# Two instead of four weight matrices converted inside attention, and a gated network whose first group runs by chunk over two tiles

## Chip, core and metric

One core of a Trainium2 chip. The metric is the device time of one execution in microseconds; the lower, the better. Three runs of the kernel before gave a median of 986.8 us.

## What is computed

Three stages follow each other on 2304 tokens of width 512 (4 batches of 512 local and 32 global tokens, 8 heads of 64):

```python
out_l = sm(where(|i-j| <= 32, scale * q_l k_l^T, -1e9) ++ scale * q_l k_g^T) @ (v_g ++ v_l)
out_g = sm(scale * q_g (k_g ++ k_l)^T) @ (v_g ++ v_l)
x = out_g ++ out_l                                     # [2304, 512]
x = (sigmoid(x @ w_gate) * (x @ w_val)) @ w_out        # d_ff = 1536
h = x @ w_in                                           # d_ff = 2048
out = (P(h) / (Q(h) + 1e-6)) @ w2_out                  # cubic over quadratic
```

The weights of both networks arrive as 64-bit floats, seen by the kernel as pairs of 32-bit words. Each 128x512 block of them (called a matrix below) is converted on the chip to a high and a low float32r part before it is used.

## The kernel before

Attention runs over 16 units (a batch and a pair of heads). Its steps stand in one table with a place for each (`STEPS`), and the order of issue is unit number plus place, sorted; every engine then works through its instructions in the order of issue. The steps of a matrix's conversion are in the same table and are run for the first `others` units, one matrix per unit: `w_raw` (the load), `w_mag` (two activations, lines 463 and 464), `w_bits` (three VectorE instructions, lines 471 to 473), `w_add` (GpSimd, line 478), `w_hi` (a cast on ScalarE, line 487) and `w_lo` (a subtraction on GpSimd, line 492). `others` is 4 (`Weights.EARLY`).

The gated network runs over 6 groups of two chunks (`G1` = 2 chunks of 128 hidden columns) and within a group over 5 tiles of tokens (two of 512, three of 384). `first(f, i)` makes gate and value of chunk `f` on tile `i`: 12 matmuls each (lines 527 to 529, the third of every three reads the low part of the weights), a sigmoid (554), the product (555), the cast `gh` (558) and the difference `gl` (559). `second(f0, i, gs)` multiplies both chunks of the group by `w_out` (lines 570 to 572) and adds to `gacc` (580 or 582). For tile `i` of a group the order is: `first` of chunk 0, `second` of the tile before, `first` of chunk 1.

Conversions of the matrices that are left run between these. `step()` issues magnitude, bits and add of the next matrix and the load of the one two further on. `finish()` issues `hi` and `lo` of all that are stepped but not yet finished. So the cast of a matrix is issued after the ScalarE instructions of the `first` that was issued before `finish()`. The converted order begins with gate 0, value 0, gate 1, value 1, out 0, out 1; the raw words, `v` and `q` have two buffers each, so the magnitude of a matrix can be written only when `lo` of the matrix two before has read its `v`.

In the trace a name such as `w11gate` is the matrix gate of network 1, chunk 1; `w11out` is that of `w_out`; `pg` and `pv` are the sums of gate and value, `p` those of `second`. `ptl` and `pth` are the low and high parts of the transposed probabilities in attention, `pspv` the sums of probabilities times values, `pss` and `psgl` the scores.

Of the kernel before, what the change touches and what calls it, by code (L numbers as in the profile page):

```python
# [32 lines left out]
TILES = [(0, 512), (512, 512), (1024, 384), (1408, 384), (1792, 384)]  # L33
# [104 lines left out]


KEPT = dict(k=4, q=3, v=2)  # L140


def attention(ctx, tc, ident, xh, xl, ins, other={}, others=0):
# [33 lines left out]
    def load(u, names="kqv"):  # L177

        b, pr = units[u]
        for x in names:  # L180
            if f"{x}n" in st[u]:
                continue
            shape = [128, NBLK, WIN] if x == "k" else [128, NBLK, 128]
            t = st[u][f"{x}n"] = two.tile(shape, F32, tag=f"{x}n", name=f"{x}n{u}", bufs=KEPT[x])
            nc.sync.dma_start(t, ins[f"{x}_l"][b, pr])
# [337 lines left out]
def layer(nc, ps, wh, wl, mh, ml):  # L523

    for k in range(4):
        w = slice(k * 128, (k + 1) * 128)
        nc.tensor.matmul(ps, wh[:, w], mh[:, k], start=k == 0, stop=False)  # L527
        nc.tensor.matmul(ps, wh[:, w], ml[:, k], start=False, stop=False)  # L528
        nc.tensor.matmul(ps, wl[:, w], mh[:, k], start=False, stop=k == 3)  # L529
# [11 lines left out]
def gated(nc, pools, xpool, wp, xh, xl):  # L541
    G = G1
    NF = FF // 128
    acc = [pools.acc.tile([128, 4, n], F32, tag=f"acc{i}", name=f"gacc{i}") for i, (_, n) in enumerate(TILES)]
    yh, yl = [None] * len(TILES), [None] * len(TILES)

    def first(f, i):
        n = TILES[i][1]
        pg = pools.ps1.tile([128, 512], F32, tag="p1", name=f"pg{f}_{i}")
        pv = pools.ps1.tile([128, 512], F32, tag="p1", name=f"pv{f}_{i}")  # L550
        layer(nc, pg[:, 0:n], *wp.have[1, f, "gate"], xh[i], xl[i])
        layer(nc, pv[:, 0:n], *wp.have[1, f, "val"], xh[i], xl[i])
        t = pools.t.tile([128, 512], F32, tag="u", name=f"t{f}_{i}")
        nc.scalar.activation(t[:, 0:n], pg[:, 0:n], AF.Sigmoid)
        nc.vector.tensor_tensor(t[:, 0:n], pv[:, 0:n], t[:, 0:n], ALU.mult)  # L555
        gh = pools.g.tile([128, 512], F32R, tag="gh", name=f"gh{f}_{i}")
        gl = pools.g.tile([128, 512], F32R, tag="gl", name=f"gl{f}_{i}")
        nc.scalar.copy(gh[:, 0:n], t[:, 0:n])  # L558
        nc.vector.tensor_tensor(gl[:, 0:n], t[:, 0:n], gh[:, 0:n].bitcast(F32), ALU.subtract)  # L559
        return gh, gl  # L560

    def second(f0, i, gs):
        n = TILES[i][1]
        ps = [pools.ps2.tile([128, 512], F32, tag="p2", name=f"p2{f0}_{i}_{m}") for m in range(4)]
        for k, (gh, gl) in enumerate(gs):
            wh, wl = wp.have[1, f0 + k, "out"]
            for m in range(4):
                w = slice(m * 128, (m + 1) * 128)
                a, z = k == 0, k == len(gs) - 1
                nc.tensor.matmul(ps[m][:, 0:n], wh[:, w], gh[:, 0:n], start=a, stop=False)  # L570
                nc.tensor.matmul(ps[m][:, 0:n], wh[:, w], gl[:, 0:n], start=False, stop=False)  # L571
                nc.tensor.matmul(ps[m][:, 0:n], wl[:, w], gh[:, 0:n], start=False, stop=z)  # L572
        final = f0 + G == NF
        if final:
            yh[i] = xpool.tile([128, 4, n], F32R, tag=f"xh{i}", name=f"yh{i}")
            yl[i] = xpool.tile([128, 4, n], F32R, tag=f"xl{i}", name=f"yl{i}")
        for m in range(4):
            a = acc[i][:, m]
            if f0 == 0:
                nc.vector.tensor_copy(a, ps[m][:, 0:n])  # L580
            else:
                nc.vector.tensor_tensor(a, ps[m][:, 0:n], a, ALU.add)  # L582
            if final:
                nc.scalar.copy(yh[i][:, m], a)
                nc.gpsimd.tensor_tensor(yl[i][:, m], a, yh[i][:, m].bitcast(F32), ALU.subtract)

    pending = None
    early, jobs = (NF // G - 1) * len(TILES) + 1, len(wp.order) - wp.done
    for f0 in range(0, NF, G):
        for i in range(len(TILES)):  # L590
            k = f0 // G * len(TILES) + i
            more = (k + 1) * jobs // early - k * jobs // early
            gs = [first(f0, i)]
            wp.finish()
            wp.step()
            if pending:
                second(*pending)
            wp.finish()
            for _ in range(more - 2):
                wp.step()  # L600
            gs += [first(f0 + k, i) for k in range(1, G)]
            pending = (f0, i, gs)
            wp.finish()
            wp.step()
            if f0 + G == NF and i > 0:
                for _ in range(2 if i % 2 else 1):
                    wp.load()

    def rest():
        second(*pending)  # L610
        wp.finish()

    return yh, yl, rest
# [154 lines left out]
@with_exitstack  # L768
def tile_kernel(ctx: ExitStack, tc, ins, out):
    nc = tc.nc  # L770
    ctx.enter_context(tc.manual_schedule())
    const = ctx.enter_context(tc.tile_pool(name="const", bufs=1))
    xpool = ctx.enter_context(tc.tile_pool(name="xpool", bufs=1))
    early = ctx.enter_context(tc.tile_pool(name="early", bufs=1))
    ident = const.tile([128, 128], F32, name="ident")
    xh = [xpool.tile([128, 4, n], F32R, tag=f"xh{i}", name=f"xh{i}") for i, (_, n) in enumerate(TILES)]
    xl = [xpool.tile([128, 4, n], F32R, tag=f"xl{i}", name=f"xl{i}") for i, (_, n) in enumerate(TILES)]
    dram = ctx.enter_context(tc.tile_pool(name="dram", bufs=1, space=bass.MemoryType.DRAM))
    wp = Weights(tc, early, dram, {"gate": ins["w_gate"], "val": ins["w_val"], "in": ins["w2_in"]},
                 {1: ins["w_out"], 2: ins["w2_out"]})  # L780

    co = const.tile([128, 8], F32, name="co")
    with ExitStack() as c:
        other = dict(w_raw=wp.fetch, w_mag=wp.magnitude, w_bits=wp.bits, w_add=wp.add, w_hi=wp.hi, w_lo=wp.lo)
        attention(c, tc, ident, xh, xl, ins, other, wp.EARLY)
    wp.done = wp.split = wp.EARLY
    for j in range(2):
        wp.fetch(wp.EARLY + j)

    nc.sync.dma_start(co[:, 0:4], ins["a"].unsqueeze(0).to_broadcast([128, 4]))  # L790
    nc.sync.dma_start(co[:, 4:6], ins["b"].unsqueeze(0).to_broadcast([128, 2]))
    with ExitStack() as c:
        wp.late = c.enter_context(tc.tile_pool(name="late", bufs=1))
        pools = Pools(c, tc)
        wp.staging = pools.t
        yh, yl, rest = gated(nc, pools, xpool, wp, xh, xl)
        rational(nc, pools, wp, yh, yl, rest, co, out)

# [60 lines left out]
```

## Time and profile before

| | |
|---|---|
| median of 3 runs | 986.8 us (986.78 to 986.83) |
| the profiled execution | 987.2 us, span of its instructions 985.3 us |
| TensorE busy | 956.4 us, 97% of the span |
| VectorE, ScalarE, GpSimd busy | 725.4, 622.4 and 556.3 us |
| attention (first score matmul to first gate matmul) | 4.78 to 177.24 us |
| gated network | 177.24 to about 614 us |
| rational network | to 985.3 us |
| mean granted TensorE clock | 0.994 of full speed |

A row of the timeline gives the start, the duration, the engine, the line, the operation, what it writes and reads, and in brackets how long the engine sat idle before it and what ended that. A matmul's duration reaches beyond the start of the next one, since matmuls are pipelined; the distance of two starts is its price.

### The profile page before, as it was taken

To read this page: it belongs to the slowest core of one execution; us is meant where nothing else is said; L and a number is where in the kernel's file an instruction comes from. 1 tells how busy PE (TensorE), PEld (TensorE's weight loads), DVE (VectorE), ACT (ScalarE), POOL (GpSimd) and SP (SyncE) were. 2 spreads that over 40 slices of the span, in tenths; PEclk is the share of its full clock that TensorE was granted. 3 is DMA by queue.
4 is the path that set the end of the run, shared out by engine and by line. 5 is a ranking of instruction groups with operands and counts; after the bars stand their busy time and mean duration, and the time that the engine had idled before them with its cause. 6 is when DMAs were issued, how large, how long until landed. Compare 5 with 4: busy or idle time off the path is not lost.

```text
span 985.3 us, 14544 instructions
## 1 busy us (share of the span) xinstructions
PE 956.4 (97%) x5024; PEld 847.7 (86%) x5024; DVE 725.4 (74%) x1324; ACT 622.4 (63%) x1272; POOL 556.3 (56%) x520
## 2 busy tenths in 40 slices
PE   5999998999999999999999999999999999999996
PEld 4778887789899899899899898888888888888895
DVE  6988887467667676677667435978788888878985
ACT  5898997434444444444444337877777777877783
POOL 4888888534445444454444336644565666656663
PEclk9999999999999999999999999999999999999998
DMA  7546453234444533444344412001300130010111
GB/s 242 165 124 177 135 162 68 81 104 154 130 143 136 169 128 118 139 150 135 126 151 146 171 44 86 1 1 44 129 1 1 65 107 1 22 65 1 65 54 65
DMA packets 56926, 98.62 MB, mean 100 GB/s; under 512 B 5396, under 2 KB 31124, under 8 KB 56852
## 3 DMA queue, kind: packets, MB, share of 16 engines
q1 hardware_dynamic: 56852, 97.69, 31.1%
q8 instruction: 40, 0.66, 0.3%
q14 instruction: 34, 0.28, 0.1%
HBM read 69.62 MB, written 21.23 MB: 92 GB/s over the span
## 4 chain that ended last, share of the span: by engine, by line
PE 77%; DVE 1%; POOL 1%; issue 1%; ACT 1%; POOLq 0%; DVEq 0%
PE rp L721 6%; PE rp L720 6%; PE rp L719 6%; PE rp L529 6%; PE rp L527 6%; PE rp L528 6%; PE pg L527 5%; PE pg L528 5%; PE pg L529 5%; PE pv L528 5%; PE pv L527 5%; PE pv L529 5%; PE p L572 4%; PE p L571 4%; PE p L570 4%
## 5 line engine op out<-in xcount | busy, mean ns | idle before, releaser
L651 POOL TENSOR_TENSOR v<-v,u 128x384 f32<-128x384 f32 (+1 forms) x80 | 96.3, 1204 | 112.3 <-ACT v L647 111.7
L694 POOL TENSOR_TENSOR rgl<-t,rgh 128x384 fp32r<-128x384 f32 (+1 forms) x80 | 96.4, 1205 | 37.4 <-POOL v L651 30.6
L558 ACT CAST gh<-t 128x384 fp32r<-128x384 f32 (+1 forms) x60 | 33.4, 557 | 124.4 <-DVE t L555 124.4
L555 DVE TENSOR_TENSOR t<-pv,t 128x384 f32<-128x384 f32 (+1 forms) x60 | 36.6, 609 | 77.6 <-PE pv L529 73.7
L659 DVE TENSOR_TENSOR t<-rp,t 128x384 f32<-128x384 f32 (+1 forms) x80 | 48.6, 607 | 54.2 <-ACT t L655 53.5
L644 ACT ACTIVATE u<-rp 128x384 f32<-128x384 f32 (+1 forms) x80 | 42.6, 532 | 65.6 <-PE rp L529 65.4
L680 DVE SCALAR_TENSOR_TENSOR v<-v,u 128x384 f32<-128x384 f32 (+1 forms) x80 | 78.9, 987 | 0.0
L684 DVE SCALAR_TENSOR_TENSOR t<-t,co,v 128x384 f32<-128x384 f32 (+1 forms) x80 | 74.0, 925 | 2.8
L559 DVE TENSOR_TENSOR gl<-t,gh 128x384 fp32r<-128x384 f32 (+1 forms) x60 | 39.5, 658 | 37.4 <-ACT gh L558 37.4
L258 ACT ACTIVATE p<-p,mx 128x224 f32<-128x224 f32 x128 | 60.6, 477 | 6.1 <-DVE mx L251 5.7
L647 ACT ACTIVATE v<-u,co 128x384 f32<-128x384 f32 (+1 forms) x80 | 60.3, 754 | 2.7
L668 ACT ACTIVATE u<-v,co 128x384 f32<-128x384 f32 (+1 forms) x80 | 52.7, 659 | 10.1 <-POOL v L651 10.0
L582 DVE TENSOR_TENSOR gacc<-p,gacc 128x384 f32<-128x384 f32 (+1 forms) x100 | 54.8, 602 | 4.6 <-PE p L572 4.6
L655 ACT ACTIVATE t<-rp,co 128x384 f32<-128x384 f32 (+1 forms) x80 | 55.8, 697 | 0.0
L334 DVE TENSOR_TENSOR ptl<-pspt,pth 112x640 fp32r<-112x640 f32 x64 | 51.0, 815 | 6.0 <-ACT pth L330 5.5
L676 DVE SCALAR_TENSOR_TENSOR v<-v,u 128x384 f32<-128x384 f32 (+1 forms) x80 | 55.3, 691 | 0.0
L325 PE MATMUL pspt<-ident,p 128*112 128x128 f32 x256 | 46.3, 281 | 6.8 <-ACT p L258 4.1
L663 DVE SCALAR_TENSOR_TENSOR t<-t,co,rp 128x384 f32<-128x384 f32 (+1 forms) x80 | 52.7, 659 | 0.0
L330 ACT CAST pth<-pspt 112x640 fp32r<-112x640 f32 x64 | 43.4, 686 | 13.6 <-PE pspt L326 13.1
L672 ACT ACTIVATE u<-u,co 128x384 f32<-128x384 f32 (+1 forms) x80 | 51.9, 649 | 0.0
L690 ACT CAST rgh<-t 128x384 fp32r<-128x384 f32 (+1 forms) x80 | 43.5, 544 | 5.6 <-DVE t L684 5.6
L251 DVE CUSTOM_DVE_ANT_0 p<-pss,masks 128x224 f32<-128x224 f32 x128 | 41.1, 382 | 6.2 <-PE pss L242 5.8
(578 smaller groups left out, 3376.1 us busy)
## 6 DMA issues: line engine op xcount, KB each, us to landing
raw2in<-in_w_in SPq DMA_DIRECT2D x16, 512.0 KB, 3.7
raw2out<-in_w_out SPq DMA_DIRECT2D x16, 512.0 KB, 3.6
kn<-in_k_l SPq DMA_DIRECT2D x16, 448.0 KB, 3.7
raw1gate<-in_w_gate SPq DMA_DIRECT2D x12, 512.0 KB, 5.5
raw1val<-in_w_val SPq DMA_DIRECT2D x12, 512.0 KB, 3.6
raw1out<-in_w_out SPq DMA_DIRECT2D x12, 512.0 KB, 3.9
out<-racc SPq DMA_DIRECT2D x17, 256.0 KB, 2.0
qn<-in_q_l SPq DMA_DIRECT2D x16, 256.0 KB, 3.7
```

Of the source, the lines that this page charges most:

```text
L258: nc.scalar.activation(p, p, AF.Exp, bias=s["mx", half][:, n : n + 1], scale=-1.0, accum_out=s["sm", half][:, n : n + 1])
L527: nc.tensor.matmul(ps, wh[:, w], mh[:, k], start=k == 0, stop=False)
L528: nc.tensor.matmul(ps, wh[:, w], ml[:, k], start=False, stop=False)
L529: nc.tensor.matmul(ps, wl[:, w], mh[:, k], start=False, stop=k == 3)
L647: nc.scalar.activation(new(u, "v"), st[u]["u"], AF.Identity, bias=b0, scale=b1)
L651: nc.gpsimd.tensor_tensor(s["v"], s["v"], s["u"], ALU.mult)
L680: nc.vector.scalar_tensor_tensor(s["v"], s["v"], 2.0, s["u"], ALU.subtract, ALU.mult)
L684: nc.vector.scalar_tensor_tensor(s["t1"], s["t1"], a0, s["v"], ALU.add, ALU.mult)
L694: nc.gpsimd.tensor_tensor(s["gl"], s["t1"], s["gh"].bitcast(F32), ALU.subtract)
L719: nc.tensor.matmul(ps, gh[:, w], wh, start=k == 0, stop=False)
L720: nc.tensor.matmul(ps, gh[:, w], wl, start=False, stop=False)
L721: nc.tensor.matmul(ps, gl[:, w], wh, start=False, stop=k == G - 1)
```

## The change

Attention converts gate 0 and value 0 alone (`CONVERTED` = 2); `Weights.EARLY`, which also says how many places of the ring lie in the early pool, stays at 4. Right behind attention, ahead of the gated network's first matmul, two `step()` issue magnitude, bits and add of gate 1 and value 1. The gated network then opens with chunk 0 on tiles 0 and 1 and chunk 1 on tiles 0 and 1, in place of both chunks tile by tile: `first(0, 0)`; `hi` and `lo` of gate 1 and value 1; `step()` of out 0 and out 1; `first(0, 1)`; `hi` and `lo` of out 0 and out 1; `step()` of the next two (gate 2 and the first of the rational network); `first(1, 0)`; `hi` and `lo` of those; one `step()`; `second` of tile 0; `first(1, 1)`. From tile 2 on the loop is as before, with the conversions that are left spread so that they run two ahead and end three tiles sooner.

```diff
+CONVERTED = 2
...
-    pending = None
-    early, jobs = (NF // G - 1) * len(TILES) + 1, len(wp.order) - wp.done
+    gs = [[], []]
+    for g in range(G):
+        for i in range(2):
+            gs[i].append(first(g, i))
+            wp.finish()
+            if g == 0:
+                wp.step()
+                wp.step()
+            if (g, i) == (G - 1, 0):
+                wp.step()
+                second(0, 0, gs[0])
+    pending = (0, 1, gs[1])
+    early, jobs = (NF // G - 1) * len(TILES) - 2, len(wp.order) - wp.done
     for f0 in range(0, NF, G):
         for i in range(len(TILES)):
-            k = f0 // G * len(TILES) + i
-            more = (k + 1) * jobs // early - k * jobs // early
+            k = f0 // G * len(TILES) + i - 2
+            if k < 0:
+                continue
+            more = min((k + 1) * jobs // early + 2, jobs) - min(k * jobs // early + 2 * (k > 0), jobs)
             gs = [first(f0, i)]
             wp.finish()
             wp.step()
-            if pending:
-                second(*pending)
+            second(*pending)
...
-        attention(c, tc, ident, xh, xl, ins, other, wp.EARLY)
-    wp.done = wp.split = wp.EARLY
+        attention(c, tc, ident, xh, xl, ins, other, CONVERTED)
+    wp.done = wp.split = CONVERTED
     for j in range(2):
-        wp.fetch(wp.EARLY + j)
+        wp.fetch(CONVERTED + j)
...
         wp.staging = pools.t
+        for _ in range(2):
+            wp.step()
```

## Rows read from the trace of the kernel before

**Rows 1.** Busy time by engine in two stretches: steady attention, gated network.

```profile
core 0: us, PE busy (x) PEld busy (x) DVE busy (x) ACT busy (x) POOL busy (x), PEclk, DMA share, GB/s
70.00:160.00 90.00, 87.83 (x629) 75.45 (x629) 77.25 (x248) 81.21 (x244) 75.54 (x105) 1.00 0.50 139
177.24:614.00 436.76, 436.36 (x2222) 398.77 (x2222) 273.46 (x447) 194.75 (x351) 196.72 (x158) 1.00 0.39 128
```

**Rows 2.** What TensorE waited for: total, times, longest, all in us.

```profile
PE pspv L343 <- DVE ptl L334: 2.6, 3, 1.8
...
PE pg L527 <- ACT xs L360: 1.2, 1, 1.2
```

**Rows 3.** Timeline of TensorE: the global scores, once in two units.

```profile
26.71 2.25 PE L280 MATMUL psgl<-kn,qgn 128*128 128x512 f32 x8
...
49.48 2.24 PE L280 MATMUL psgl<-kn,qgn 128*128 128x512 f32 x8
...
70.10 2.24 PE L280 MATMUL psgl<-kn,qgn 128*128 128x512 f32 x8
...
147.64 2.24 PE L280 MATMUL psgl<-kn,qgn 128*128 128x512 f32 x8
```

**Rows 4.** Timeline of TensorE around its waits in units 2 to 5.

```profile
37.98 0.45 PE L343 MATMUL pspv<-pth,vb 112*128 112x320 f32 x2
40.26 0.41 PE L343 MATMUL pspv<-ptl,v 112*128 112x320 f32 x1 [1.83 <-DVE ptl L334]
...
41.69 3.36 PE L242 MATMUL pss<-kn,qn 64*128 64x224 f32 x16
...
52.23 0.56 PE L343 MATMUL pspv<-pth,v 112*128 112x320 f32 x2 [0.50 <-DVE ptl L334]
...
63.01 1.78 PE L242 MATMUL pss<-kn,qn 64*128 64x224 f32 x16
```

**Rows 5.** Timeline of VectorE: the bits of gate 1, then a low part.

```profile
36.55 0.40 DVE L471 TENSOR_SCALAR v1gate<-v1gate 128x512 f32<-128x512 f32 x1
36.98 1.04 DVE L472 TENSOR_SCALAR v1gate<-v1gate 128x512 uint32<-128x512 uint32 x1
38.05 1.41 DVE L473 SCALAR_TENSOR_TENSOR v1gate<-raw1gate,v1gate 128x512 uint32<-128x512 uint32 x1
39.39 0.81 DVE L334 TENSOR_TENSOR ptl<-pspt,pth 112x640 fp32r<-112x640 f32 x1
```

**Rows 6.** TensorE busy and its granted clock (third value) in stretches of 2 us.

```profile
38.00:40.00 2.00, 0.43 (x3) 1.00 0.53 123
...
42.00:44.00 2.00, 2.00 (x12) 0.50 0.56 213
...
179.00:181.00 2.00, 2.00 (x10) 1.00 0.00 0
```

**Rows 7.** Timeline of TensorE: `second` of tile 0, both chunks.

```profile
193.73 0.39 PE L570 MATMUL p<-gh,w10out 128*128 128x512 f32 x1
...
196.68 0.39 PE L571 MATMUL p<-gl,w11out 128*128 128x512 f32 x1
197.28 0.50 PE L572 MATMUL p<-gh,w11out 128*128 128x512 f32 x1 [0.22 <-POOL w11out L492]
```

**Rows 8.** Timelines of VectorE, ScalarE and GpSimd: first product, then out 0's conversion.

```profile
183.11 0.69 DVE L555 TENSOR_TENSOR t<-pv,t 128x512 f32<-128x512 f32 x1 [6.70 <-PE pv L529]
...
185.09 0.42 DVE L471 TENSOR_SCALAR v1out<-v1out 128x512 f32<-128x512 f32 x1
...
183.83 0.62 ACT L558 CAST gh<-t 128x512 fp32r<-128x512 f32 x1 [1.50 <-DVE t L555]
184.36 0.67 ACT L463 ACTIVATE v1out<-raw1out 128x512 f32<-128x512 f32 x1
...
188.17 0.62 ACT L487 CAST w10out<-v1out 128x512 fp32r<-128x512 f32 x1 [2.57 <-POOL v1out L478]
...
186.85 1.29 POOL L478 TENSOR_TENSOR v1out<-v1out,q1out 128x512 uint32<-128x512 uint32 x1 [6.21 <-DVE v1out L473]
188.87 1.29 POOL L492 TENSOR_TENSOR w10out<-v1out,w10out 128x512 fp32r<-128x512 f32 x1 [0.73 <-ACT w10out L487]
```

More of the change, by code (lines that the diff above doesn't have):

```diff
@@ L600, in gated @@
                 wp.step()
-            gs += [first(f0 + k, i) for k in range(1, G)]
+            gs += [first(f0 + g, i) for g in range(1, G)]
             pending = (f0, i, gs)
```

## The prediction

> **What bounds the kernel now.** I read the profile in this order: TensorE's waits, the granted clock and busy time by stretch, then the timelines around the two places that the edit touches. The windows by stage show that TensorE sets the pace: it is busy 87.83 of 90 us in steady attention and 436.36 of 436.76 us in the gated network, while VectorE, ScalarE and GpSimd stay at 75 to 81 us of the 90 [rows 1]. So work that is taken off those three engines is worth only what TensorE waits for it, and work that is put on them costs only what TensorE comes to wait. The list of TensorE's waits names the ones in attention that can belong to a conversion: 2.6 us on the low parts `ptl` from VectorE, 1.8 us of it in one piece [rows 2].
>
> **What attention gives back.** The global scores come once in two units, so the distance of their starts is the price of two units. From 70.10 to 147.64 us there are four such distances: 77.54 / 4 = 19.39 us each. The distance from 26.71 to 49.48 is 22.77, that from 49.48 to 70.10 is 20.62 [rows 3]. These two hold the conversions of gate 1 and value 1, and they are 3.38 and 1.23 us above the steady price, together 4.6 us. The timeline says what fills the first. TensorE waits 1.83 us for a `ptl` until 40.26, and soon after the 16 score matmuls at 41.69 take 3.36 us, against 1.78 us at 63.01: another 1.58 us [rows 4]. VectorE is why: the bits of gate 1 stand from 36.55 to 39.39, 2.84 us, right ahead of that `ptl` in its queue [rows 5]. The slow scores are the clock: half speed is granted from 42 to 44 us, right after a stretch of 2 us in which TensorE was busy for 0.43 [rows 6]. In the second distance a wait of 0.50 us for VectorE at 52.23 is visible [rows 4]; the rest of its 1.23 us I can't put down to one row. Removing both conversions takes away two magnitudes, two times three bits, two adds, two casts and two subtractions, and two loads from SP's queue. I give the loads no price: among the conversions' waits on TensorE's list it is `ptl` alone that stands for more than a microsecond [rows 2]; if a load had held units 2 to 5, its share is within the 4.6 us already.
>
> Bounds: at most the whole 4.6 us; at least 3.0, if the clock still falls once in there for some other wait (4.6 less 1.58). The `hi` and `lo` of gate 0 and value 0 still lie in the first distance, so I take 3.4 us of the first and 0.7, somewhat over half, of the second: **4.1 us**.
>
> **What the opening costs.** Before, TensorE ran the opening almost without a wait: `second` of tile 0 lost 197.28 - 196.68 = 0.60 less one pitch of 0.23 (2.95 us for 13 matmuls from 193.73), **0.4 us**, for `lo` of out 1 [rows 7]. That wait goes, since out 1 is now a pass of 5.4 us earlier. TensorE's number of matmuls is unchanged, and so are its starts up to `second` of tile 0 at 193.73, unless something is late. So I follow the conversions in the order of issue, with hand-overs from one view [rows 8]: product to cast 0.72 (183.11 to 183.83), cast to ScalarE's next 0.53, magnitude to bits 0.73 (184.36 to 185.09), bits to add 1.76 (185.09 to 186.85), cast to subtraction 0.70 (188.17 to 188.87), add and subtraction 1.29 each.
>
> The two `step()` ahead of the network cost nothing: ScalarE's next instruction there is the first sigmoid, VectorE sits idle 6.70 us until 183.11, and the bits, from about 178, fit even at 2.84 us each within half a microsecond [rows 5, 8]. GpSimd's two adds end near 184.5 at the latest.
>
> From the first cast `gh` at 183.83: casts of gate 1 and value 1 at 184.36 and 184.89, their subtractions from 185.06 to 187.64. First needed at 188.3 by `first(1, 0)`: ready, no wait. The magnitude of out 0 needs the buffer that gate 1's subtraction frees at 186.35, so it starts at 186.4, that of out 1 at 187.64. Bits of out 0 from 187.13, of out 1 until 190.65, both ahead of the product of `first(0, 1)` in VectorE's queue; so that product starts at 190.65, though its sums were there at 188.5. Its cast 191.37, casts of out 0 and out 1 at 191.90 and 192.43, subtractions from 192.60 to 195.18. `second` needs the first at 194.18 and has it at 193.9: ready, with 0.3 us to spare.
>
> Now the next two are stepped, and this is where it gets late. Their magnitudes wait for the two subtractions and start at 193.9 and 195.2; their bits run from 194.63 to 198.15, and behind them in VectorE's queue stands the product of `first(1, 0)`, whose sums are ready at 194.0. So product 198.15, cast `gh` 198.87, difference `gl` 199.57 to 200.26. TensorE has done chunk 0 of `second` by then and wants `gh` at 196.45 and `gl` at 196.68: it goes on with `gl` at 200.3, **3.6 us late**.
>
> The one price that moves this is the bits: four of them stand in the chain, one behind another. At 1.76 us the delay is 3.6; with the hand-over of some 0.2 us left out, 2.9; at the 2.84 us that gate 1's bits took beside GpSimd's full queue [rows 5], 7.9. Beside each of the four GpSimd has one or two operations of 1.29 us, so I take 1.86, near the quiet row: **4.0 us**, and 2.9 to 5.2 for the range.
>
> The Trainium skill ("GPSIMD Engine Reference", Specifications) says that GpSimd shares its SBUF interfaces with VectorE and that they get in each other's way for VectorE instructions in a two-port mode or with two SBUF inputs. The 2.84 us beside the 1.76 agree with it; taken for all four bits it would make the opening 7.9 us late and the sum +4.7 instead of +0.8.
>
> **The clock.** That wait is one piece of some 2.5 us and another of 0.5. After 1.83 us of waiting the clock fell to half (1.2 instead of 2.4 GHz) and 1.58 us were lost; after 1.2 us, at the start of the gated network, it did not fall [rows 2, 4, 6]. The new wait is longer than the one that cost a fall. Bounds 0 and 1.6 us; part of a slow stretch may lie in the rest of the wait, so I take **1.3 us**.
>
> **What costs nothing.** Chunks and tiles in another order need no more buffers: at most three `gh` and `gl` live at once. Conversions that end three tiles sooner mean about three in each tile of some 14 us, as already half of the tiles have now, and TensorE was never short there [rows 1]. If that cover were gone, a late product would cost one bits, 1.8 us, per tile.
>
> **Sum**: -4.1 - 0.4 + 4.0 + 1.3 = **+0.8 us**. The profiled execution took 987.2 us (span 985.3), 0.4 above the median of the runs; on the median, 986.8 + 0.8 = **987.6 us**.
>
> **Rivals.** What a measurement here can tell from no change is about 0.2%, 2 us.
>
> Forecast, the wait and one fall of the clock: 52%, from 985.9 to 990.2 by the bounds above, mostly within 2 us.
>
> The wait, but the clock holds: -0.5, 986.3 us, 20%. For it: nothing fell after 1.2 us; against it: it fell after 1.83. The Trainium skill ("TensorE: Matmul & The Clock Gate", Why this matters for your kernels) warns only of gaps longer than either piece of this wait; by that rule this case is the right one, but the 1.83 us row doesn't agree with it.
>
> Faster: the product of `first(1, 0)` is not held up by the bits ahead of it. Then attention's gain stands alone: -4.1 - 0.4 = -4.5, 982.3 us, 12%. It is decided by whether VectorE gets to that product before about 195.3; it turns the sign beyond 2 us as soon as the delay with its clock is under 2.5 us. Against it: three engines hand each matrix on, and the magnitudes must wait for buffers. For it: one buffer freed sooner than I followed shortens the chain by 1.3 us.
>
> Slower, and the change does not do what it says: attention gives back about 2 us, because GpSimd (75.54 of 90 us in the steady part [rows 1]) or the two conversions that stay hold TensorE instead; with the rest as forecast +2.9, 989.7 us, 16%.
>
> The range takes in the forecast's bounds, the held clock and most of the slower case, and leaves out most of the faster one: 984.8 to 990.2 us. Faster by over 0.2%: the faster rival and a little of the second, 0.15. Slower: four fifths of the slower rival and a quarter of the forecast, 0.27. Within: 0.58.
>
> **What would show it.** In attention the wait at 40 us and the slow scores gone, the distances near 19.4 to 20 us, and the first gate matmul near 173 instead of 177.24. In the opening one new wait of TensorE, on `gh` or `gl` of chunk 1 of tile 0, with VectorE's bits of the next two matrices right before the product, then half clock. Gate 1's and value 1's weights never waited for. Wrong would be: the score distances unchanged; `second` of tile 0 without a wait; or a wait for the weights themselves.

## The result, and the profile after

The kernel after takes 991.3 us (991.18 to 991.63, 4 runs) against 986.8 us (984.8 to 986.83, 4 runs): slower by 4.6 us from median to median. The ratio of the runs is 1.0054, interval 1.0042 to 1.0066, which is 4.1 to 6.5 us. The forecast was 987.6 us, within 984.8 to 990.2. The profiled execution took 991.31 us with a span of 989.5 us, 4.2 us more than the span of 985.3 us before.

First TensorE's waits in the kernel after, in the gated network: total, times and longest, in us.

```profile
PE p L574 <- ACT gh L562: 3.9, 1, 3.9
PE pv L531 <- ACT t L558: 1.3, 2, 1.1
PE pg L531 <- ACT xs L364: 1.2, 1, 1.2
PE p L576 <- POOL w10out L496: 0.4, 1, 0.4
PE p L575 <- DVE gl L563: 0.2, 1, 0.2
```

Before, the same stretch had the 1.2 us for `xs` [rows 2] and 0.22 us for out 1 [rows 7], no more. The waits for `gh` and `gl` are the one forecast. The second line, value sums that wait for a sigmoid, was not in the forecast at all. Next the timeline of TensorE in the kernel after (in these functions a line of the changed kernel has a number higher by 4).

```profile
26.26 2.24 PE L284 MATMUL psgl<-kn,qgn 128*128 128x512 f32 x8
...
45.83 2.25 PE L284 MATMUL psgl<-kn,qgn 128*128 128x512 f32 x8
...
65.32 2.24 PE L284 MATMUL psgl<-kn,qgn 128*128 128x512 f32 x8
...
173.07 0.50 PE L531 MATMUL pg<-xh,w10gate 128*128 128x512 f32 x1 [1.16 <-ACT xs L364]
...
189.79 0.39 PE L575 MATMUL p<-gl,w10out 128*128 128x512 f32 x1
190.60 0.50 PE L576 MATMUL p<-gh,w10out 128*128 128x512 f32 x1 [0.43 <-POOL w10out L496]
...
192.77 0.39 PE L576 MATMUL p<-gh,w10out 128*128 128x512 f32 x1
197.04 0.50 PE L574 MATMUL p<-gh,w11out 128*128 128x512 f32 x1 [3.88 <-ACT gh L562]
197.77 0.64 PE L575 MATMUL p<-gl,w11out 128*128 128x512 f32 x1 [0.23 <-DVE gl L563]
...
201.20 0.49 PE L574 MATMUL p<-gh,w11out 128*128 128x512 f32 x1
...
201.99 0.39 PE L531 MATMUL pg<-xh,w11gate 128*128 128x512 f32 x1
...
237.07 0.44 PE L531 MATMUL pv<-xh,w10val 128*128 128x384 f32 x1 [1.05 <-ACT t L558]
...
250.74 0.50 PE L531 MATMUL pv<-xh,w12val 128*128 128x512 f32 x1 [0.23 <-ACT t L558]
```

Put beside the same matmuls of before, these rows give the whole ledger.

- **Attention, -4.17 us.** The first gate matmul comes at 173.07 instead of 177.24, where the second stretch of [rows 1] begins. The first two distances of the global scores are 19.57 and 19.49 us instead of 22.77 and 20.62 [rows 3], 4.33 us less; the wait of 1.83 us and the slow scores after it [rows 4] are gone. The next distance is half a microsecond longer than before (65.32 to 84.99 is 19.67, 70.10 to 89.23 was 19.13), and 0.45 us was ahead already at 26.26 (26.71 before), where no conversion differs.
- **Opening, +6.48 us.** From the first gate matmul to `first(1, 1)` of tile 1 it takes 201.99 - 173.07 = 28.92 us instead of 199.68 - 177.24 = 22.44. The distances say where: 190.60 - 189.79 = 0.81 for low parts of out 0, 0.58 above a pitch of 0.23, and 0.11 in the step behind it; 197.04 - 192.77 = 4.27 for `gh`, 4.04 above; 197.77 - 197.04 = 0.73 for `gl`, 0.50 above. These are 5.2 us of waiting. Then eight steps from 197.77 to 201.20 take 3.43 us instead of 8 x 0.227 = 1.82, and the three behind them 0.09 more than their pitch: 1.7 us for the clock. Together 6.9, less the 0.4 that the wait for out 1 cost before.
- **Later, +1.84 us.** At 237.07 the distance to the matmul of before jumps from +2.31 to +3.64 within two steps, at 250.74 from 3.64 to 4.15, and it stays there.

Sum: -4.17 + 6.48 + 1.84 = +4.15 us, the 4.2 us of the spans.

VectorE in the kernel after, in the opening, shows why the wait is longer than forecast.

```profile
182.90 0.81 DVE L475 TENSOR_SCALAR v1out<-v1out 128x512 f32<-128x512 f32 x1 [1.89 <-ACT v1out L467]
183.74 0.43 DVE L476 TENSOR_SCALAR v1out<-v1out 128x512 uint32<-128x512 uint32 x1
...
185.27 1.40 DVE L476 TENSOR_SCALAR v1out<-v1out 128x512 uint32<-128x512 uint32 x1
...
187.31 0.69 DVE L559 TENSOR_TENSOR t<-pv,t 128x512 f32<-128x512 f32 x1
...
191.28 0.80 DVE L475 TENSOR_SCALAR v1gate<-v1gate 128x512 f32<-128x512 f32 x1 [1.88 <-ACT v1gate L467]
...
193.65 1.37 DVE L476 TENSOR_SCALAR v2in<-v2in 128x512 uint32<-128x512 uint32 x1
...
195.66 0.68 DVE L559 TENSOR_TENSOR t<-pv,t 128x512 f32<-128x512 f32 x1
```

Twice a pair of bits stands right ahead of a product (`t<-pv,t`): 182.90 to 187.31 is 4.41 us, 191.28 to 195.66 is 4.38 us, 2.20 us for each matrix. In each pair the second L476 takes 1.40 or 1.37 us where the first took 0.43, and the first L475 takes 0.8 us where the second takes 0.42. GpSimd's timeline says what ran beside them: the add of the matrix before beside the long L476, a subtraction beside the long L475.

```profile
185.07 1.32 POOL L482 TENSOR_TENSOR v1out<-v1out,q1out 128x512 uint32<-128x512 uint32 x1 [1.64 <-DVE v1out L477]
...
190.51 1.30 POOL L496 TENSOR_TENSOR w11out<-v1out,w11out 128x512 fp32r<-128x512 f32 x1
...
193.44 1.28 POOL L482 TENSOR_TENSOR v1gate<-v1gate,q1gate 128x512 uint32<-128x512 uint32 x1 [1.64 <-DVE v1gate L477]
```

Both long L476 end when that add ends (185.07 + 1.32 = 186.39 against 185.27 + 1.40 = 186.67; 194.72 against 195.02), within 0.3 us. Without the two lengthenings, 0.39 and 0.97 us, the first pair would have taken 3.05 us, 1.52 for each matrix. The kernel before shows the same throughout its gated network: its L471 took 0.42 or 0.43 us for the 15 of 64 matrices where GpSimd was idle, and 0.63 to 1.00 us for the 49 where GpSimd was at work. The windows of the same stretch carry the clock, which falls after the wait.

```profile
core 0: us, PE busy (x) PEld busy (x) DVE busy (x) ACT busy (x) POOL busy (x), PEclk, DMA share, GB/s
196.00:198.00 2.00, 0.73 (x2) 0.41 (x3) 1.03 (x2) 1.63 (x3) 1.58 (x2) 1.00 0.48 136
198.00:200.00 2.00, 2.00 (x6) 1.51 (x6) 0.39 (x1) 1.13 (x3) 2.00 (x2) 0.50 0.81 286
```

ScalarE's timeline in the kernel after explains both kinds of waits.

```profile
190.58 0.67 ACT L467 ACTIVATE v1gate<-raw1gate 128x512 f32<-128x512 f32 x1 [0.89 <-POOL w10out L496]
...
196.37 0.62 ACT L562 CAST gh<-t 128x512 fp32r<-128x512 f32 x1 [2.81 <-DVE t L559]
...
234.91 0.62 ACT L491 CAST svout<-v2out 128x512 fp32r<-128x512 f32 x1 [3.18 <-POOL v2out L482]
235.44 0.66 ACT L467 ACTIVATE v1out<-raw1out 128x512 f32<-128x512 f32 x1
...
236.55 0.47 ACT L558 ACTIVATE t<-pg 128x384 f32<-128x384 f32 x1
```

In the opening the magnitude waits for the buffer that the low part of out 0 frees. At 235 us a cast (`hi` of a matrix) waits 3.18 us for GpSimd's add. Behind it in the queue stand another magnitude and then the sigmoid of chunk 1. The sums of gate and value share three PSUM buffers in turn, so the value sums of the next tile take the one that this sigmoid reads; it ends at 237.02, TensorE goes on at 237.07.

A cast that waits 3.18 us is not enough by itself. The same cast of the kernel before waits as long and costs TensorE nothing:

```profile
230.34 0.62 ACT L487 CAST svout<-v2out 128x512 fp32r<-128x512 f32 x1 [3.18 <-POOL v2out L478]
230.87 0.48 ACT L554 ACTIVATE t<-pg 128x384 f32<-128x384 f32 x1
```

TensorE is 2.31 us later in the kernel after, but this cast is 4.57 us later and the sigmoid 5.68. So ScalarE has fallen 2.26 us further behind, after a tile with four conversions instead of three, and the magnitude between cast and sigmoid adds 1.1.

### The profile page after: what moved, and what is told of

Its sections match the earlier page's. It is cut to its first block, busy times and chain, and to the rows that moved or that the text cites. A ratio compares the mean times of both kernels' runs of the same rounds, so it can differ in the third digit from the quotient of the medians.

```text
span 989.5 us, 14548 instructions
## 1 busy us (share of the span) xinstructions
PE 956.7 (97%) x5024; PEld 847.1 (86%) x5024; DVE 728.5 (74%) x1324; ACT 623.8 (63%) x1272; POOL 555.4 (56%) x520
## 4 chain that ended last, share of the span: by engine, by line
PE 82%; DVE 7%; POOL 5%; issue 2%; ACT 2%; DMA 1%; SPq 0%; POOLq 0%; DVEq 0%; ACTq 0%
PE rp L738 6%; PE rp L737 6%; PE rp L736 6%; PE rp L533 6%; PE rp L531 6%; PE rp L532 6%; PE pspv L347 5%; PE pv L531 4%; PE pv L533 4%; PE pv L532 4%; PE p L575 4%; PE pg L531 4%; PE pg L533 4%; PE p L576 4%; PE pg L532 4%; PE p L574 4%
## 5 line engine op out<-in xcount | busy, mean ns | idle before, releaser
L589 POOL TENSOR_TENSOR yl<-gacc,yh 128x384 fp32r<-128x384 f32 (+1 forms) x20 | 22.8, 1175 | 51.5 <-ACT yh L588 51.5
```

## Experiments

The theory was: the opening's loss is the place of the next two matrices' bits in VectorE's queue, the later loss is the denser start of the conversions that are left. Rivals: the opening's loss comes from the magnitudes' two buffers; the order by chunk costs by itself; or the weights come too late once attention converts only two. All ratios are against the kernel before on the same chip: 986.6 us for the first three experiments and for the order by chunk alone, 985.5 us for the other four.

**The next two not stepped in the opening.** The steps ahead of `first(1, 0)` go; the spread of the rest takes those two matrices in.

```diff
-            if g == 0:
+            if (g, i) == (0, 0):
                 wp.step()
                 wp.step()
```

> The changed kernel without the two step() behind first(0, 1), so gate 2 and the first matrix of the rational network are not converted in the opening. Theory: TensorE's wait of 3.9 us in second of tile 0 comes from their bits standing ahead of the product of first(1, 0) in VectorE's queue; without them that wait and the half-speed stretch behind it are gone, the wait of 0.4 us for the low part of out 0 stays; time 983 to 985 us, the rest depending on the later waits on the sigmoid. Rival: the wait comes from the four weight matrices themselves (gate 1 to out 1 converted too late), then at least 2 us of it stay and the time stays above 987.

984.57 us, ratio 0.9985 (0.9976 to 0.9994). The wait for `gh` is gone and TensorE's clock holds through the opening; the waits for out 0 (0.43) and for the sigmoid (1.06 at 229.45, 0.23 later) stay. The span is 981.9 us, 7.6 less than in the kernel after: 4.04 + 0.50 + 1.7 = 6.24 from the ledger, and 1.35 because its first gate matmul already comes at 171.72 (more on that at the end). Without the two steps there is neither the wait nor the fall of the clock.

**Conversions spread evenly.** The two ahead are given up and the conversions end where they did before the change, the opening stays as it is. ("Three tiles sooner" was too much: the term `early` fell by three, but tiles are now counted from the third one on. In the trace the last magnitude comes at 525.03 us instead of 542.47, some one and a half tiles sooner.)

```diff
-    early, jobs = (NF // G - 1) * len(TILES) - 2, len(wp.order) - wp.done
+    early, jobs = (NF // G - 1) * len(TILES) - 1, len(wp.order) - wp.done
...
-            more = min((k + 1) * jobs // early + 2, jobs) - min(k * jobs // early + 2 * (k > 0), jobs)
+            more = (k + 1) * jobs // early - k * jobs // early
```

> The changed kernel with its opening, but the conversions behind it spread evenly over 24 tiles (2, 2, 3, 2, 3 per tile) instead of two ahead (4, 3, 2, 3, 2). Theory: the two later waits of TensorE on the sigmoid (1.05 and 0.23 us at 237 and 251 us, some 1.9 us with what goes with them) come from the denser start; they vanish, 989.4 us. Rival: they are the backlog that the opening leaves on ScalarE; then they stay, 991.3 us.

989.02 us, ratio 1.003 (1.0017 to 1.0044), against 1.0054 of the kernel after. TensorE's waits in the gated network:

```profile
PE p L574 <- ACT gh L562: 3.9, 1, 3.9
PE pg L531 <- ACT xs L364: 1.2, 1, 1.2
PE p L576 <- POOL w10out L496: 0.4, 1, 0.4
PE p L575 <- DVE gl L563: 0.2, 1, 0.2
```

The line of the sigmoid is gone and all others stay. The ratios differ by 2.4 us; from the first gate matmul to the end of the span it is 814.3 us against 816.4, 2.1 less; the ledger has 1.84.

**Both.** Both edits at once.

> Both edits at once: no step() behind first(0, 1), conversions behind the opening spread evenly. Theory: attention's 4.2 us are kept and nothing of size is paid for them: 982.5 to 983.2 us. Rival: work taken out of the opening comes back as late weights or late sigmoids in group 0 or 1: above 984.5.

983.10 us, ratio 0.9972 (0.9962 to 0.9981). Its first gate matmul comes at 173.03, as in the kernel after, so the spans compare directly: 982.3 against 989.5, 7.2 us less. The ledger has 6.24 + 1.84 = 8.1, less two new waits of 0.22, which take 0.5 each in the distances. The two losses add up; with both removed the change is worth some 3 us over the kernel before.

**The next two behind, not left out.** The same two steps, issued behind `first(1, 0)` and its cast instead of ahead of it; the single `step()` there goes, and conversions are spread evenly.

```diff
-            if g == 0:
+            if i == 0:
                 wp.step()
                 wp.step()
             if (g, i) == (G - 1, 0):
-                wp.step()
                 second(0, 0, gs[0])
```

> The opening does the same conversions as the changed kernel but one, with the two step() of gate 2 and of the first matrix of the rational network issued behind first(1, 0) instead of behind first(0, 1); even spread behind the opening. Theory: the wait of 3.9 us is a matter of place in VectorE's and ScalarE's queues: behind the product and the cast of first(1, 0) the same bits hold nothing up, no wait on gh, 982.5 to 983.5 us. Rival: the three engines have too much to do in the opening wherever it stands; then a wait of 2 us or more stays in the opening and the time is above 985.

982.99 us, ratio 0.9969 (0.9956 to 0.9982). VectorE in its opening:

```profile
190.37 0.69 DVE L559 TENSOR_TENSOR t<-pv,t 128x512 f32<-128x512 f32 x1 [0.82 <-ACT t L558]
...
192.43 0.41 DVE L475 TENSOR_SCALAR v1gate<-v1gate 128x512 f32<-128x512 f32 x1
...
195.83 0.69 DVE L477 SCALAR_TENSOR_TENSOR v2in<-raw2in,v2in 128x512 uint32<-128x512 uint32 x1
```

The bits of the same two matrices now run behind the product, which comes at 190.37 instead of 195.66, and take 4.0 us (192.43 to 196.44; 4.4 in the kernel after). TensorE waits for nothing in chunk 1 of `second` (192.95, then 193.18). From the first gate matmul to the end of the span it takes 808.4 us, against 816.4 in the kernel after and 808.1 before the change. So it is the place in the queue, not the work.

**A third buffer for the magnitudes.** The rival of the buffers, on the kernel after.

```diff
-        v = self.early.tile([128, 512], U32, tag="v", name=f"v{net}{i}{f}", bufs=2)
+        v = self.early.tile([128, 512], U32, tag="v", name=f"v{net}{i}{f}", bufs=3)
```

> The changed kernel with three buffers for the magnitude v instead of two. Theory: half of the opening's lateness is magnitudes that wait for a subtraction on GpSimd to free their buffer; the bits of the next two then end some 2.2 us sooner and the wait on gh is 1.5 to 2 us instead of 3.9; time 987.1 to 989.2 us, the lower with the clock staying up. Rival: the buffers don't matter, VectorE's queue alone does; wait 3.9 us, 991 us.

989.35 us, ratio 1.0039 (1.0024 to 1.0054): no more than a microsecond or two, with intervals that overlap those of the kernel after. The wait for `gh` is still 3.58 us, far from the 1.5 to 2 expected. The magnitude of gate 2 does come earlier, 187.88 instead of 190.58; 1.47 us of that is an earlier first gate matmul (171.60), 1.23 us is the buffer's. VectorE shows what took more than half of that back:

```profile
188.64 0.48 DVE L475 TENSOR_SCALAR v1gate<-v1gate 128x512 f32<-128x512 f32 x1 [0.96 <-ACT v1gate L467]
189.15 1.40 DVE L476 TENSOR_SCALAR v1gate<-v1gate 128x512 uint32<-128x512 uint32 x1
...
191.66 1.37 DVE L476 TENSOR_SCALAR v2in<-v2in 128x512 uint32<-128x512 uint32 x1
...
193.67 0.68 DVE L559 TENSOR_TENSOR t<-pv,t 128x512 f32<-128x512 f32 x1
```

The bits now start while GpSimd still makes low parts, so the first L476 is long as well as the second, and the pair takes 188.64 to 193.67 = 5.0 us instead of 4.4. The product is issued behind them as before and comes 0.5 us earlier, counted from the first gate matmul; up to the end of the span 0.8 us is won. The buffers decide when the bits start, not that they stand in the way.

**Both, with the third buffer.**

> The kernel with both edits mended, and three buffers for v. Theory: the wait of 0.4 us for the low part of out 0 goes, 0.4 us below that kernel. Rival: no difference, since other waits of 0.2 us stay.

983.46 us, ratio 0.9977 (0.9967 to 0.9986), no difference to two buffers (0.9972). The wait for out 0 is 0.17 instead of 0.43 us; that much is below what these runs can tell.

**The order by chunk alone.** Four conversions in attention as before (`CONVERTED` = 4), the opening by chunk without the two `step()`, conversions spread evenly.

> The opening by chunk alone: four matrices converted in attention as before, out 0 and out 1 stepped ahead of the gated network, no further step() in the opening until second, even spread behind it. Theory: the first gate matmul is back at 177.2 us and the order by chunk costs nothing by itself: 986.2 to 986.9 us. Rival: the order by chunk costs or gains by itself: more than 1 us away from 986.8.

986.42 us, ratio 1.0006 (0.9997 to 1.0016): no difference. The wait for `ptl` is back (2.0 us in 3 waits, 1.3 the longest) and the distances of the global scores are 22.43 and 20.57 us again. In the gated network two waits of 0.22 us are left beside that for `xs`. The first gate matmul comes at 175.22, not at 177.2 as expected, since the first of these scores already come at 24.85 (26.71 before); from there it is 150.4 us, 150.5 before and 146.8 in the kernel after. So the order by chunk costs nothing and gives nothing by itself, and 3.6 us of what attention gives back do come from the two conversions.

**Two conversions in attention, tile by tile.** The loop of before, with attention's part of the change and the two `step()` behind it.

> Attention's part of the change alone: two matrices converted in attention, gate 1 and value 1 stepped ahead of the gated network, opening tile by tile and spread as before the change. Theory: attention gains 4.2 us; TensorE then waits about 3 us for the low part of gate 1 right behind first(0, 0), and the clock falls after it: 987 to 989 us. Rival: the wait is short because the steps are issued ahead of the network; then 983 us or less, and the order by chunk would not have been needed.

986.43 us, ratio 1.0006 (0.9996 to 1.0015). TensorE waits for the weights:

```profile
179.68 0.50 PE L527 MATMUL pg<-xh,w11gate 128*128 128x512 f32 x1 [2.01 <-ACT w11gate L487]
...
181.03 0.50 PE L529 MATMUL pg<-xh,w11gate 128*128 128x512 f32 x1 [0.62 <-POOL w11gate L492]
```

The waits are near the 3 us expected; the fall of the clock did not come (see the end), and the time is just below the 987 to 989 expected. From the first gate matmul to the end of the span it takes 811.3 us, 3.2 more than before: what attention gives back is lost again for gate 1, which the old order needs one pass earlier. The order by chunk is what covers it: with the next two behind, on the same chip, it is 0.9969 against 1.0006, 3.7 us.

## Why the prediction was wrong, step by step

**Right: what attention gives back.** Forecast -4.1 (3.0 to 4.6), measured -4.17, with the wait and the slow scores gone as named. The 0.45 us that were ahead at 26.26 are in it, so the conversions' own share is nearer 3.7; the wait of 0.4 us for out 1 went as forecast.

**Right: where the opening waits, and for what.** `gh` of chunk 1 of tile 0, late because the bits of the next two stand ahead of its product; removing the steps removes the wait, and moving them behind the product does so too. The rival "faster" needed that product ahead of the bits; the mended versions have it, and come out some 3 us below the kernel before, not its 4.5, with the wait for out 0 still there.

**Mis-sized: the wait, 5.2 us instead of 4.0.** The formula held, its price did not. It gave 3.6 us at 1.76 for one matrix and grew by four times what one matrix takes longer. With the measured 2.20: 3.6 + 4 x 0.44 = 5.4, and 5.2 was measured (0.69 of it for out 0, which I had ready with 0.3 us to spare, since the same longer bits stood ahead of its cast too). I had seen 2.84 us beside GpSimd and 1.76 without [rows 5, 8] and took 1.86, near the quiet row, though the chain itself puts the add of one matrix beside the bits of the next, and though its quiet row is one of the 15 in 64 where GpSimd was idle. The Trainium skill ("GPSIMD Engine Reference", Specifications) warns that GpSimd and VectorE get in each other's way over shared SBUF interfaces. The trace agrees, 0.43 us becoming 1.40 beside an add of 1.32. The extreme that I had put beside it, 2.84 for all four, was too much: one L475 and one L476 of each pair are hit.

**Mis-sized, a little: the clock, 1.7 instead of 1.3 us.** It fell to half once, after the wait, as forecast, and the upper bound of 1.6 was near it. The piece of "some 2.5 us" that I gave the clock does not follow from my chain: there `gh` is written at 198.87 + 0.62 = 199.49, 3.0 us after TensorE wants it, and more at 1.86 a matrix. 3.88 was measured. The rival of a held clock leaned on the shorter piece. The Trainium skill ("TensorE: Matmul & The Clock Gate", Why this matters for your kernels) warns of long gaps. The 3.88 us here agree with it; the clock also fell after 1.83 us before [rows 4, 6] and after 1.27 us with four conversions in attention, which that section does not name.

**Failed: "What costs nothing".** I had put conversions two ahead and ending sooner at nothing, because three in a tile occurred before as well, and named 1.8 us per tile through a late product if that cover were gone. In the trace the first two tiles behind the opening carry four and three conversions (three and two before), and 1.84 us were lost; with an even spread these waits are gone. The way was another one: not a product behind bits on VectorE, but a sigmoid on ScalarE, behind a cast that waits for GpSimd's add and a magnitude more, on an engine that the fourth conversion had put behind. I had looked at TensorE's busy share and the mean count of conversions, not at what stands behind a waiting cast in the densest tile.

Together the three sizes were +1.2, +0.4 and +1.84, 3.4 us on a forecast of +0.8, which gives the +4.2 of the spans. The range ended at +3.4: 3.0 from attention, the wait at 5.2, the clock at 1.6. Wait and clock came out at about those bounds. It is the conversions later on, with no bound above nothing, that took the time out of the range: -4.17 + 6.48 = +2.3 without them, and 989.0 us measured with the even spread.

## What to carry to other kernels

When work is put into an engine's queue, ask which instruction of the bound engine's chain stands behind it there, and issue the work behind that one: the same two steps cost 6.2 us ahead of a product, with the clock that fell after it, and nothing behind it. Where a chain over three engines repeats, price its links beside each other, not from a row where one stood alone. A step costed at nothing needs its waits followed on every engine that it is issued to, for the densest tile and not for the mean.

## What the runs showed that was not expected

**A wait's length does not settle whether the clock falls.** With two conversions in attention and the loop of before, TensorE's waits of 2.01 and 0.62 us stand within 4 us, and the clock holds:

```profile
178.00:180.00 2.00, 0.32 (x1) 0.30 (x2) 1.15 (x2) 1.51 (x3) 1.43 (x2) 1.00 0.65 205
180.00:182.00 2.00, 1.38 (x6) 0.84 (x5) 0.28 (x1) 1.14 (x3) 2.00 (x2) 1.00 0.10 41
182.00:184.00 2.00, 2.00 (x10) 1.62 (x10) 1.64 (x3) 0.25 (x1) 0.36 (x2) 1.00 0.00 0
```

With four conversions in attention and the order by chunk, a busier stretch of 2 us, with a wait of 1.27 us until 38.03, is followed by half clock:

```profile
36.00:38.00 2.00, 0.76 (x4) 0.50 (x4) 2.00 (x3) 2.00 (x8) 2.00 (x3) 1.00 0.65 148
38.00:40.00 2.00, 1.97 (x10) 1.60 (x12) 1.62 (x4) 1.96 (x8) 1.83 (x3) 0.77 0.72 167
40.00:42.00 2.00, 2.00 (x12) 1.83 (x12) 1.73 (x5) 1.88 (x6) 2.00 (x2) 0.50 0.92 356
```

What tells the two apart stays open; each is one execution.

**The start varies by some 1.5 us between executions.** The first global scores take 3.38 us in the profile of the kernel after and 2.39 us in that with an even spread, with the same instructions up to there:

```profile
8.12 3.38 PE L284 MATMUL psgl<-kn,qgn 128*128 128x512 f32 x8
```

```profile
8.16 2.39 PE L284 MATMUL psgl<-kn,qgn 128*128 128x512 f32 x8
```

The next global scores then come at 26.26 and 24.82, and the first gate matmul at 173.07 and 171.66. In the ten traces, one for each version, these scores come at 24.8 to 25.2 us in five and at 26.25 to 26.74 in five. That this makes much of the 2.6 us over which the runs of one and the same kernel are spread (984.7 to 987.3 in 26 runs of the kernel before) is likely and not shown. A single span tells two versions apart only beyond that, and stages are better compared from the first gate matmul on. The clock's column shows full speed in both, so that it is the clock is only inferred from the durations, which are near those at half speed (3.36 against 1.78 us for the 16 score matmuls in [rows 4]); what sets the moment was not tried.
